# The load of the last two z1 tiles is queued on GpSimd behind the accumulating store of the fourth output tile

## The chip, the cores and the metric

The kernel runs on one NeuronCore of a Trainium2 chip, in one launch. The metric is the time of the program on the device in microseconds; of several runs the median is given. Five engines work side by side, each through its own instructions in order: TensorE (PE, matmuls and transposes, with its weight loads shown as PEld), VectorE (DVE), ScalarE (ACT), GpSimd (POOL) and SyncE (SP). SP only issues transfers here; ACT and POOL issue some as well. All transfers (DMAs) run on 16 DMA engines. What SP issues is on queue 1 of the profile, what POOL issues on queue 0.

## The reference

```python
def ref(x, wqkv, w_phi, wo, w_in, w_sp, b_sp, w_out):   # x: 1 x 2048 x 512, 32 heads of 16, FH = 688
    xn = layernorm(x)
    # A: linear attention with a learned feature map
    q, k, v = split_heads(xn @ wqkv)
    phi = lambda t: concat(softmax(t @ w_phi), softmax(-(t @ w_phi)))
    kv, z = phi(k).T @ v, sum(phi(k))
    a = (phi(q) @ kv) / (phi(q) @ z + 1e-6)
    # B: gated MLP that mixes over the sequence
    zz = gelu(xn @ w_in)
    z1, z2 = zz[..., :688], layernorm(zz[..., 688:])
    g = w_sp @ z2 + b_sp                                 # 2048 x 2048 times 2048 x 688
    b = (z1 * g) @ w_out
    return x + a @ wo + b
```

All is float32. The kernel splits each float32 operand of a matmul into a rounded part and a rest ("h" and "l") and does three matmuls (lines L57, L58, L59) for one.

## The kernel before

The sequence is cut into 16 tiles of 128 rows (NT = 16), taken in pairs for the mixing over the sequence (NP = 8 pairs).

The first part normalizes and transposes x, projects q, k, v and the first half of z (`z1_raw`), and puts the unfinished z1 (before its gelu) and the features of q to DRAM (`z1_d`, `e_d`). The second part makes z2. The third, up to about 486 us of the profile, multiplies `w_sp` with z2 pair by pair (tiles `g`); `drain` (L805 to L810) puts the sums together, and `gate` takes the gelu of the pair's z1 (L819), multiplies (L822), and returns a function `turn` that transposes the product in blocks (L831, L833) and stores it to DRAM as `u_d` and `ur_d` (L837, L839), from SP except for pair 6, where it is POOL. `load_z1` (L787) fetches a pair's z1: two transfers of 344 KB, issued on POOL. The last pair (7, tiles 14 and 15) is drained at the end of this part, but gated only in the middle of the next.

The last part, the loop over i = 0, 2, ..., 14 at the end of the function, makes the output tiles, two in a turn:

- `fetch_u` and `gated` bring u of a tile back (L855, L856) and split it on ACT and DVE (`uh`, `ul`); `project_u` multiplies it with `w_out` (tiles `wu`) into the PSUM tile `pout` (its last two matmuls are L1018).
- `load_q` brings the features of a q tile (`et`, L557); `features` ends them on DVE (`q_fin`, L564 to L571, with a last multiply L571); up to tile 7 the matrix engine transposes them (`ptq`, L989), from tile 8 on DVE does it in blocks and they go through DRAM (`q_d`, L580 and L582).
- `attend` multiplies with `kvT` (`po`, L1004) and splits the result (`oT`, first half on ACT, rest on DVE); `project_o` multiplies it with `wo` into the same `pout`, copies it to `xr` on ACT (L1040) and adds it to the output in DRAM with an accumulating store on POOL (L1041). x itself was put there earlier.
- before the loop, SP issues the loads of `kvT` (L972), of `wo` in 16 pieces of 64 KB (L850, tiles `wof`, rounded to `woh` and `wol`), and then `et` of tile 3, u of tiles 2 and 3, and `et` of tile 4.

After the turn i = 2 the z1 of the last pair is loaded, and after i = 6 (`GATE_LAST`) that pair is gated; its u is needed by the last turn.

The order of each engine's instructions is written by a scheduler that reckons with the times of instructions and transfers; the program text is only its input, so an instruction can come earlier than its place in the text. `with tc.issue_after(ins)` adds an edge: instructions of the block that are on the same engine as `ins` are put behind `ins` in that engine's order. It adds no wait on another engine. `lasts` is a list of remembered instructions for such edges; `lasts[6]` is read at one place only, the load of the last pair's z1.

Of the kernel before, what the change touches and what calls it, by code (L numbers as in the profile page):

```python
# [13 lines left out]
ALU = mybir.AluOpType  # L14
# [27 lines left out]
def mixer(ctx: ExitStack, tc: tile.TileContext, x, x_t, wv, wqkT, phi_bd, wo, w_in, wst, b_r, w_out, out):  # L42
    nc = tc.nc
    pe, act, dve, pool, sp = nc.tensor, nc.scalar, nc.vector, nc.gpsimd, nc.sync
# [10 lines left out]
    def mm3(dst, a, b, start, stop):  # L55
        (ah, al), (bh, bl) = a, b
        pe.matmul(dst, ah, bh, start=start, stop=False)  # L57
        pe.matmul(dst, ah, bl, start=False, stop=False)  # L58
        return pe.matmul(dst, al, bh, start=False, stop=stop).ins  # L59
# [500 lines left out]
    def q_fin(et, tmp, zb):  # L560

        e, r, t, w = et[:, :NF], *(et[:, NF + k * 2 * H:NF + (k + 1) * 2 * H] for k in range(3))
        den = et[:, NF + 6 * H:QW]
        dve.tensor_tensor(tmp, e, zb, op=ALU.mult)  # L564
        dve.tensor_reduce(t, heads(tmp), axis=AX.X, op=ALU.add)
        dve.tensor_tensor(t, t, r, op=ALU.mult)
        dve.scalar_tensor_tensor(den, pairs(t, 0), EPS_DEN, pairs(t, 1), op0=ALU.add, op1=ALU.add)
        dve.reciprocal(den, den)
        dve.tensor_tensor(w.rearrange("p (h a) -> p h a", a=2), r.rearrange("p (h a) -> p h a", a=2),
                          den.unsqueeze(2).to_broadcast([P, H, 2]), op=ALU.mult)  # L570
        return e, dve.tensor_tensor(heads(e), heads(e), bc(w, 2 * H), op=ALU.mult).ins  # L571
# [6 lines left out]
    def turn_q(s, dst, e, eng):  # L578

        dve.transpose(dst.rearrange("p (m c t) -> p m c t", c=NB, t=BL), e.rearrange("p (c m j) -> p m c j", c=NB, j=BL))  # L580
        for b in range(P // BL):
            eng.dma_start(q_d[s, :, b * QB:(b + 1) * QB].rearrange("(m j) w -> j m w", j=BL),  # L582
                          dst[b * BL:(b + 1) * BL].rearrange("p (m w) -> p m w", w=QB))
# [154 lines left out]
    for s in range(NT):  # L738
# [8 lines left out]
        for k, q in p:  # L747
            ins = act.activation(z[(slice(None), *k)], q, AF.Gelu_apprx_tanh, scale=r_x[:, s:s + 1]).ins
# [95 lines left out]
    def slot(name, dt=F32):  # L844
        return xz_tile(2 * FH, dt, name)
# [28 lines left out]
    lasts, wu = [None] * 9, []  # L874
# [67 lines left out]
    def er_pair(name):  # L942
        return cw.tile([P, 2, NF], F32, tag="er", bufs=3, name=name)

    def features(s):
        with tc.issue_after(fin[-1]):
            tmp = slot("qtmp")[:, :NF]
            es[s], ins = q_fin(ets.pop(s), tmp, zb)
        fin.append(ins)
        if s >= TQ:  # L950
            if s % 2 == 0:
                ft[s] = er_pair("f")
            turn_q(s, tmp, es.pop(s), pool)
            brought[s] = sp.dma_start(ft[s - s % 2][:, s % 2], q_d[s]).ins
            return
        lasts[6] = ins

    def gated(u):
        return split_u(*u, wk.tile([P, KF, P], F32R, tag="uh", name="uh"), wk.tile([P, KF, P], F32R, tag="ul", name="ul"))
# [61 lines left out]
    def project_o(i, oT, p):  # L1021
        ts = slice(i % 2 * P, (i % 2 + 1) * P)
        rows = slice(i * P, (i + 1) * P)
        xr = wk.tile([P, D], F32, tag="xr", bufs=3, name="xr")
        if i >= NT - 2:
            sp.dma_start(xr, x[rows, :])
        if i == NT - 1:
            dve.tensor_tensor(xr, p, xr, op=ALU.add)
            parts = [(slice(k * D // 2, (k + 1) * D // 2), pst.tile([P, D // 2], F32, tag="tr", name="pend")) for k in range(2)]
        else:  # L1030
            parts = [(slice(0, D), p)]
        for cs, q in parts:
            for c in range(ND):
                lasts[4] = mm3(q, (oT[0][:, c, ts], oT[1][:, c, ts]), (wo_h[:, c, cs], wo_l[:, c, cs]),
                               q is not p and c == 0, c == ND - 1)
            if i == NT - 2:
                dve.tensor_tensor(xr, p, xr, op=ALU.add)
                sp.dma_start(out[rows, :], xr)
            elif q is p:
                act.activation(xr, p, AF.Copy)  # L1040
                ins = pool.dma_start(out[rows, :], xr, accum_op=ALU.add).ins  # L1041
                tc.add_manual_dep(ins, seeds[i].name, mybir.DependencyInfo(
                    mybir.DependencyClass.Sync, mybir.DependencyReason.DATA), reason="out holds x")
            else:
                dve.tensor_tensor(xr[:, cs], q, xr[:, cs], op=ALU.add)
                sp.dma_start(out[rows, cs], xr[:, cs])
# [8 lines left out]
    with tc.issue_after(lasts[0]), tc.issue_after(lasts[1]), tc.issue_after(fin[-1]):  # L1055
        for c in range(ND):
            rows = [(m * QP, (m + 1) * QP) for m in range(c // 2 * 8 + c % 2, (c // 2 + 1) * 8, 2)]
# [7 lines left out]
    def ahead(i):  # L1065

        if i + 5 < NT:
            ets[i + 5] = load_q(i + 5, slot("et"))
        if i + 4 < NT:
            with tc.issue_after(brought[i + 2]) if i + 6 >= NT else ExitStack():  # L1070
                us[i + 4] = fetch_u(i + 4)
        if 3 < i + 3 < NT:
            features(i + 3)

    p, nxt = {}, dict(enumerate(uT))
    for i in range(0, NT, 2):
        p[i] = project_u(i, nxt.pop(i))
        if 0 < i < NT - 2:
            nxt[i + 2] = gated(us.pop(i + 2))
        with tc.issue_after(lasts[2]):  # L1080
            oT = attend(fT)
        with tc.issue_after(lasts[3]):
            p[i + 1] = project_u(i + 1, nxt.pop(i + 1))
        if not i:
            fin.append(lasts[7])
            features(3)
            with tc.issue_after(fin[-1]), tc.issue_after(lasts[8]):
                nxt[2] = gated(us.pop(2))
        if i < NT - 2:
            with tc.issue_after(fin[-1]) if not i else ExitStack():  # L1090
                nxt[i + 3] = gated(us.pop(i + 3))
        for k in range(2):
            project_o(i + k, oT, p.pop(i + k))
            ahead(i + k)
        if i == 2:
            with tc.issue_after(lasts[6]):
                z = load_z1(NP - 1)
        if i == GATE_LAST:
            with tc.issue_after(lasts[0]), tc.issue_after(lasts[1]):
                gate(NP - 1, cb, z, z, gt.tile([P, 2, FU], F32, tag="zt", name="zt"))()  # L1100
            p2.close()
        if i + 2 < NT:
            with tc.issue_after(lasts[4]):
                fT = attend_T(i + 2)
# [33 lines left out]
```

## Time and profile before

| | us |
|---|---|
| median of 3 runs | 617.96 |
| lowest and highest of them | 616.56, 618.06 |
| the profiled execution, its own time | 615.26 |
| its span, first to last instruction | 613.6 |
| z1 load of the last pair issued on POOL | 479.41 and next |
| last products of the third part end, first `pout` starts | 486.81 |
| accumulating store of tile 3 issued on POOL | 520.53 |
| gelu of the last pair on ACT | 546.53 |
| last `po` group on PE starts | 599.35 |

The granted TensorE clock was 1.000 of full speed over the whole span. Times in the profile are microseconds from the span's start. A row of the timeline gives start, length, engine, line, operation, the tile written and the tile read, the number of like instructions in a row, and in brackets how long the engine had been idle before it and what ended that. A row of the waits gives who waited for whom, the total, how often, and the longest. "POOL out" with L1041 is the accumulating store, "POOL z1t" with L787 the load in question.

### The profile page before, as it was taken

To read this page: it belongs to the slowest core of one execution; us is meant where nothing else is said; L and a number is where in the kernel's file an instruction comes from. 1 tells how busy PE (TensorE), PEld (TensorE's weight loads), DVE (VectorE), ACT (ScalarE), POOL (GpSimd) and SP (SyncE) were. 2 spreads that over 40 slices of the span, in tenths; PEclk is the share of its full clock that TensorE was granted. 3 is DMA by queue.
4 is the path that set the end of the run, shared out by engine and by line. 5 is a ranking of instruction groups with operands and counts; after the bars stand their busy time and mean duration, and the time that the engine had idled before them with its cause. 6 is when DMAs were issued, how large, how long until landed. Compare 5 with 4: busy or idle time off the path is not lost.

```text
span 613.6 us, 11385 instructions
## 1 busy us (share of the span) xinstructions
PE 606.3 (99%) x4286; PEld 551.5 (90%) x4286; DVE 519.9 (85%) x930; ACT 259.9 (42%) x414; POOL 132.4 (22%) x231
## 2 busy tenths in 40 slices
PE   8999999999999999999999999999999999999997
PEld 7888888888888999999999999999999978777776
DVE  5999999999988588999989897787779979999932
ACT  5653334423433547887434443332435243332220
POOL 4122232333111014542000002001100131053440
PEclk9999999999999999999999999999999999999999
DMA  8557776666547848001454746455566798599882
GB/s 309 196 135 170 224 174 183 153 161 171 134 120 206 275 155 308 2 1 35 150 135 133 193 100 182 132 158 145 162 179 215 239 312 253 150 293 278 222 221 67
DMA packets 57950, 107.85 MB, mean 176 GB/s; under 512 B 12392, under 2 KB 24552, under 8 KB 57672
## 3 DMA queue, kind: packets, MB, share of 16 engines
q1 hardware_dynamic: 43656, 65.22, 34.5%
q0 software_dynamic: 11936, 36.28, 24.0%
q10 hardware_dynamic: 2304, 5.64, 2.4%
q8 instruction: 33, 0.54, 0.4%
q14 instruction: 21, 0.17, 0.1%
HBM read 66.85 MB, written 35.54 MB: 167 GB/s over the span
## 4 chain that ended last, share of the span: by engine, by line
PE 83%; DVE 6%; DMA 6%; issue 2%; SPq 1%; ACT 1%; POOL 0%; ACTq 0%; DVEq 0%; POOLq 0%
PE g L57 8%; PE g L58 8%; PE g L59 8%; PE proj L58 7%; PE proj L57 7%; PE proj L59 7%; PE zps L58 6%; PE zps L59 6%; PE zps L57 6%; PE pout L57 5%; PE pout L59 5%; PE pout L58 5%; DVE A L53 2%; DMA wf<-in_wst 1%; PE po L1004 1%
## 5 line engine op out<-in xcount | busy, mean ns | idle before, releaser
L57 PE MATMUL g<-B,A 128*128 128x344 f32 x448 | 142.5, 319 | 0.3 <-DVE c L810 0.3
L58 PE MATMUL g<-B,A 128*128 128x344 f32 x448 | 142.4, 319 | 0.0
L59 PE MATMUL g<-B,A 128*128 128x344 f32 x448 | 138.9, 318 | 0.0
L57 PEld LDWEIGHTS g<-B,A 128*128 128x128 f32 x448 | 84.0, 188 | 0.9 <-DVE c L810 0.6
L58 PEld LDWEIGHTS g<-B,A 128*128 128x128 f32 x448 | 84.0, 188 | 0.0
L59 PEld LDWEIGHTS g<-B,A 128*128 128x128 f32 x448 | 83.6, 188 | 0.0
L49 ACT ACTIVATE A<-S 128x512 fp32r<-128x512 f32 x64 | 39.4, 628 | 70.7 <-DVE S L622 52.3
L57 PE MATMUL proj<-wqk_h,xT 128*128 128x512 f32 x128 | 50.1, 391 | 0.0
L59 PE MATMUL proj<-wqk_h,xT 128*128 128x512 f32 x128 | 49.8, 389 | 0.0
L58 PE MATMUL proj<-wqk_l,xT 128*128 128x512 f32 x128 | 49.8, 389 | 0.0
L125 ACT ACTIVATE e<-e,r_x 128x1024 f32<-128x1024 f32 x26 | 29.8, 1149 | 42.3 <-DVE e L124 41.3
L53 DVE TENSOR_TENSOR A<-S,A 128x512 fp32r<-128x512 f32 x64 | 43.0, 684 | 3.0 <-ACT A L49 2.8
L49 ACT ACTIVATE A<-wf 128x512 fp32r<-128x512 f32 (+1 forms) x64 | 32.8, 515 | 28.1 <-DMA wf<-in_wst 15.8
L57 PE MATMUL zps<-w1h,xT 128*128 128x344 f32 (+2 forms) x128 | 40.8, 320 | 0.0
L59 PE MATMUL zps<-w1h,xT 128*128 128x344 f32 (+2 forms) x128 | 40.7, 318 | 0.0
L58 PE MATMUL zps<-w1l,xT 128*128 128x344 f32 (+2 forms) x128 | 40.7, 318 | 0.0
L57 PE MATMUL zps<-w2h,xT 128*128 128x344 f32 (+2 forms) x128 | 40.7, 318 | 0.0
L58 PE MATMUL zps<-w2l,xT 128*128 128x344 f32 (+2 forms) x128 | 40.6, 317 | 0.0
L59 PE MATMUL zps<-w2h,xT 128*128 128x344 f32 (+2 forms) x128 | 40.3, 317 | 0.0
L53 DVE TENSOR_TENSOR A<-wf,A 128x512 fp32r<-128x512 f32 (+1 forms) x64 | 35.1, 550 | 4.1 <-ACT A L49 4.0
L787 POOL DMA_DIRECT2D z1t<-z_d x16 | 8.7, 550 | 132.5 <-DMA wf<-in_wst 98.1
L128 DVE TENSOR_REDUCE sm<-e 128x64 f32<-128x1024 f32 x26 | 31.1, 1199 | 2.5 <-ACT e L125 2.5
(219 smaller groups left out, 1434.4 us busy)
## 6 DMA issues: line engine op xcount, KB each, us to landing
wf<-in_wst SPq DMA_DIRECT2D x64, 256.0 KB, 3.4
e_d<-e POOLq DMA_DIRECT2D x16, 544.0 KB, 5.0
et<-e_d SPq DMA_DIRECT2D x16, 544.0 KB, 7.6
z_d<-z1f ACTq DMA_DIRECT2D x16, 344.0 KB, 3.1
z1t<-z_d POOLq DMA_DIRECT2D x16, 344.0 KB, 4.6
zacc<-e POOLq DMA_DIRECT2D x10, 512.0 KB, 4.8
u<-u_d SPq DMA_DIRECT2D x15, 320.0 KB, 5.8
xt<-in_x SPq DMA_DIRECT2D x16, 256.0 KB, 4.4
```

The source lines that it names most:

```text
L49: return act.activation(h, src, AF.Copy).ins
L53: return (eng or dve).tensor_tensor(l, src, h.bitcast(F32), op=ALU.subtract).ins
L57: pe.matmul(dst, ah, bh, start=start, stop=False)
L58: pe.matmul(dst, ah, bl, start=False, stop=False)
L59: return pe.matmul(dst, al, bh, start=False, stop=stop).ins
L125: softmax_pair.last = less, act.activation(e, e, AF.Exp, scale=scale).ins
L128: dve.tensor_reduce(sm, heads(e), axis=AX.X, op=ALU.add)
L787: pool.dma_start(t[:, k, :FH], z1_d[2 * i + k])
L1004: lasts[3] = pe.matmul(po[r][c * QP:(c + 1) * QP, k], kvT[rows, m // 2, cols], fs[m // 4][rows, m // 2 % 2], start=True, stop=True).ins
```

## The change

The remembered instruction `lasts[6]` is no longer the last one of `features` (a multiply on DVE) for the q tiles below 8, but the accumulating store of `project_o` (on POOL). At the place where it is read, after the turn i = 2, the latest such store is that of output tile 3, the fourth. The two transfers of the z1 load are thereby queued on POOL behind that store. Nothing else differs.

```diff
     def features(s):
         with tc.issue_after(fin[-1]):
             tmp = slot("qtmp")[:, :NF]
             es[s], ins = q_fin(ets.pop(s), tmp, zb)
         fin.append(ins)
         if s >= TQ:
             ...
             return
-        lasts[6] = ins

     def project_o(i, oT, p):
             ...
             elif q is p:
                 act.activation(xr, p, AF.Copy)
-                ins = pool.dma_start(out[rows, :], xr, accum_op=ALU.add).ins
+                lasts[6] = ins = pool.dma_start(out[rows, :], xr, accum_op=ALU.add).ins
                 tc.add_manual_dep(ins, seeds[i].name, ...)

         # the place where it is read, unchanged
         if i == 2:
             with tc.issue_after(lasts[6]):
                 z = load_z1(NP - 1)
```

## Prediction

> **What bounds the kernel now.** I read the page's busy shares first, then the list of waits of the matrix engine, then the chain of work that ended last over the stretch where it leaves the matrix engine, then the queues of GpSimd and SyncE in that stretch.
>
> ```profile
> PE 606.3 (99%) x4286; PEld 551.5 (90%) x4286; DVE 519.9 (85%) x930; ACT 259.9 (42%) x414; POOL 132.4 (22%) x231
> PE ptq L989 <- DVE et L571: 1.0, 1, 1.0
> PE pout L57 <- ACT oT L49: 0.2, 1, 0.2
> PE pout L57 <- DVE c L810: 0.2, 1, 0.2
> ```
>
> The first row is of the page: matmul is busy 606.3 of 613.6 us. The other three are all the waits of the matrix engine (total, times, longest) between 475 us and the end. The changed transfer can act only there, so everything that can be won in the tail is 1.0 + 0.2 + 0.2 = 1.4 us, unless an order of instructions changes. The chain of work that ended last (start, length, what) goes through the longest of the three:
>
> ```profile
> 479.66 0.42 SPq L856
> ...
> 480.17 6.96 DMA kvT<-kvT_d
> ...
> 491.71 0.43 SPq L850
> ...
> 492.24 6.33 DMA et<-e_d
> ...
> 498.58 1.24 DVE qtmp L564
> ...
> 502.24 1.24 DVE et L571
> ...
> 503.52 1.53 PE ptq L989 x12
> ```
>
> Read backwards: the transposes `ptq` of query tiles 2 and 3 wait for `features(3)` (lines L564 to L571 on VectorE), that for the load `et` of tile 3, that for its turn on SyncE's queue behind the last pieces of `wo` (L850), and those for the landing of `kvT`, which took 6.96 us for 256 KB. So a slow stretch of the transfers between 480 and 487 us is passed on to the matrix engine at 503.5. Here is what was under way:
>
> ```profile
> 479.41 1.07 POOL L787 DMA_DIRECT2D z1t<-z_d  x2 [23.89 <-DVE ul_rt L53]
> 490.01 2.35 POOL L837 DMA_DIRECT2D u_d<-z1t  x4 [9.53 <-DVE z1t L833]
> SPq L850 <- DMA u<-u_d: 2.4, 1, 2.4
> SPq L850 <- DMA kvT<-kvT_d: 0.4, 1, 0.4
> SPq L850 <- DMA u<-ur_d: 0.3, 1, 0.3
> z1t<-z_d POOLq DMA_DIRECT2D x2, 344.0 KB, 5.9
> q0 software_dynamic: 160, 0.70, 24.6%
> ```
>
> The first two rows are of GpSimd in order of time, the next three the waits of SyncE's queue between 479 and 488 us, the last two the transfers of the same 9 us (issues with their median us to landing; then a queue's packets, MB and share of the 16 engines). Queue 0 is GpSimd's: its 160 packets are the two z1 loads, 0.70 MB. SyncE stood 2.4 + 0.3 + 0.4 = 3.1 us before its L850 loads, waiting for three earlier loads to land. Within 482 to 485 us alone:
>
> ```profile
> q0 software_dynamic: 141, 0.63, 60.6%
> q1 hardware_dynamic: 266, 0.35, 33.2%
> ```
>
> The z1 loads had 60.6% of the engines' time while SyncE's loads (queue 1) had 33.2%.
>
> **The change part by part.**
>
> The edge that is removed. It tied the z1 load to the last multiply of `features(6)`, an instruction of VectorE; the load is issued on GpSimd.
>
> ```profile
> 520.17 1.22 DVE L571 TENSOR_TENSOR et<-et 128x1024 f32<-128x1024 f32 x1
> ```
>
> That multiply (the fifth in order from tile 2's) starts at 520.17, 41 us after the load was issued at 479.41: the old edge holds nothing back. Removing it costs and brings 0.
>
> The edge that is added. Now the accumulating store of output tile 3 is the instruction remembered, and it is on GpSimd, as the load is.
>
> ```profile
> 520.53 0.86 POOL L1041 DMA_DIRECT2D out<-xr  x1 [0.78 <-ACT xr L1040]
> 535.84 0.60 POOL L582 DMA_DIRECT2D q_d<-qtmp  x1 [14.45 <-DVE qtmp L580]
> 546.53 1.34 ACT L819 ACTIVATE z1t<-z1t 128x1376 f32<-128x1376 f32 x1
> ```
>
> So both issues move from 479.41 to 520.53 + 0.86 = 521.4, past eight stores of `u_d`/`ur_d` (from 490.01; they wait for VectorE's transposes, not for the load) and four output stores. The two issues cost GpSimd 1.07 us there, inside 14.45 us in which it idles: 0. What is queued behind is the `q_d` store at 535.84, 13 us after them. With the 5.9 us to landing seen above, z1 is there at about 528.4; its only reader in wait is the gelu at 546.53, 18 us later: 0. Without that cover ScalarE would stop at the gelu, and behind it `xr` of tiles 6 and 7, `uh` and `oT`, which feed the matrix engine.
>
> What leaves 479 to 486 us. 24.6% of 9 us is 2.2 us of all 16 engines. From below: 0, if SyncE's loads landed no sooner without it. From above: the whole 2.2 us (SyncE's 3.1 us of waits leave room). I take the part that lies in 482 to 485, just ahead of the landings that SyncE waited for: 60.6% of 3 us = 1.8 us. Then the last L850 and `et` of tile 3 are issued 1.8 us earlier, at 490.4.
>
> What that is worth. These rows decide:
>
> ```profile
> 495.09 0.63 ACT L49 ACTIVATE woh<-wof 128x512 fp32r<-128x512 f32 x1 [2.63 <-DMA wof<-in_wo]
> 496.36 1.28 DVE L53 TENSOR_TENSOR oT<-po,oT 128x512 fp32r<-128x512 f32 x2
> 498.58 1.23 DVE L564 TENSOR_TENSOR qtmp<-et,zb 128x1024 f32<-128x1024 f32 x1 [0.94 <-DMA et<-e_d]
> 501.89 0.60 PE L989 MATMUL ptq<-ident,et 128*128 128x128 f32 x4
> 503.52 1.53 PE L989 MATMUL ptq<-ident,et 128*128 128x128 f32 x12 [1.04 <-DVE et L571]
> ```
>
> With its 6.33 us to landing unchanged, `et` is there at 490.4 + 6.3 = 496.7. VectorE is then free at 497.64 (496.36 + 1.28) less what the last `woh` gains; that rounding waited 2.63 us for a `wo` piece, of the same queue, so it moves by the same 1.8 us and VectorE is free at 495.8. `features(3)` starts at 496.7 in place of 498.58, ends at 501.7 in place of 503.48, and the matrix engine, which reaches the second group of transposes at 501.89 + 0.60 = 502.5, no longer waits: 1.04 us. The same earlier `woh` lets `oT` be rounded earlier, which ends the 0.18 us in which `pout` waited for it (the second wait of the list). If only `et` came sooner and `oT` not, the gain would be VectorE's 0.94 us; if nothing came sooner, 0. The third wait, 0.2 us for L810, is a drain of the matrix engine's own products and stays.
>
> What is late next. After 503.5 VectorE has no pause until 586, so it could be the next to hold the matrix engine up:
>
> ```profile
> 510.00:586.00 76.00, 76.00 (x483) 59.92 (x484) 74.45 (x112) 24.00 (x40) 25.10 (x39) 1.00 0.84 237
> 513.99 0.63 DVE L53 TENSOR_TENSOR oT<-po,oT 128x512 fp32r<-128x512 f32 x1
> 514.83 0.39 PE L59 MATMUL pout<-woh,oT 128*128 128x512 f32 x1
> ```
>
> The first row is a stretch of 76 us with the busy times of PE, PEld, DVE, ACT, POOL: VectorE 74.45. The other two show the low part of `oT` ready at 514.62 and first used at 514.83, a margin of 0.2 us. VectorE's run of work starts with `features(3)`, so it moves forward by 1.8 us while the matrix engine moves by 1.2: the margin holds. It would be lost, and the gain cut to what VectorE gained plus 0.2, if `features(3)` moved by less than 1.0.
>
> What arrives at 521 to 528 us. The 2.2 us of transfers now compete with `et` loads of tiles 10 and 11 and the stores of output tiles 2 and 3:
>
> ```profile
> 530.00:535.00 5.00, 5.00 (x24) 4.09 (x23) 4.90 (x8) 0.98 (x2) 0.00 (x0) 1.00 0.11 39
> 519.03 2.62 SPq L557 DMA_DIRECT2D et<-e_d  x2
> 538.96 1.22 DVE L564 TENSOR_TENSOR qtmp<-et,zb 128x1024 f32<-128x1024 f32 x1
> ```
>
> The transfer engines are 0.11 busy between 530 and 535, so the queue is empty again soon after, and `et` of tile 10, issued at 519.03, is first read at 538.96. A delay of 2.2 us is hidden: 0. That cover is 20 us less a landing of some 7.
>
> [...] GpSimd's issue moves into the stretch where VectorE is 74.45 of 76 us busy. The stores issued there between 495 and 530 us, by this row of L1041, landed after:
>
> ```profile
> DMA to landing us min/median/max: 6.5/7.4/9.3
> ```
>
> By the longest, z1 lands at 521.9 + 9.3 = 531.2, still 15 us ahead of the gelu, and the sum stays. [...]
>
> **The sum.** 1.04 + 0.18 = 1.22 us off the profiled execution's own 615.26 (span 613.6), so 614.04, or 0.20%. The median of the runs shown is 617.96, 2.7 us above the profiled execution; 0.2% off it is 616.75, forecast as 616.8.
>
> **The rivals.**
>
> First, nothing is won: the loads on SyncE's queue land as before, because they are bound by something else than the z1 packets, or `et` issued at 490.4 now shares the engines with the `u_d` stores from 490.01 and lands at 498.5 again; or the scheduler leaves the load where it is. For it: those stores are in flight there. Against it: 60.6% in 482 to 485, and only 1 us of the 1.8 is needed. Time 617.96.
>
> Second, slower, by one mechanism: the gate of the last z1 pair on VectorE is put at another place. The order of instructions comes from a scheduler that reckons with times, and z1 now becomes ready 42 us later.
>
> ```profile
> 550.67 1.58 DVE L822 TENSOR_TENSOR z1t<-z1t,c 128x1376 f32<-128x1376 f32 x1
> 554.41 0.32 DVE L833 STREAM_TRANSPOSE zt<-z1t 128x192 f32<-128x192 f32 x1
> 560.14 1.28 DVE L53 TENSOR_TENSOR oT<-po,oT 128x512 fp32r<-128x512 f32 x2
> ```
>
> The block from 550.67 to 554.73, 4.1 us with what lies between, is now early in its iteration. Put just ahead of the next `oT` (560.14), it delays the matrix engine by up to 4.1 less a margin like the 0.2 above, 3.9; with the 1.2 won, +2.7: 620.7. It decides from 1.2 us of delay on. Against it: the gelu is queued behind `uh` of tile 9 in both kernels, and z1 is there before that in both.
>
> [...]
>
> **How the numbers follow.** Forecast 0.65, nothing won 0.22, the gate moved 0.10, GpSimd held up 0.03. The forecast's own range is 0.9 to 1.4 us, 616.5 to 617.1, and the runs before scatter from 616.56 to 618.06, so a median may lie 1.3 us lower: 615.2. Upwards the range takes in nothing won (617.96) and the third rival: 618.6. Outside it is the second, 0.10, and some scatter. About 0.3% (1.85 us) is what a measurement of this kernel can tell from no change: faster means under 616.1, which the forecast reaches with scatter in about 3 of 10 cases, 0.2; slower is the second rival, 0.1; the rest, 0.7.
>
> **What would show it.** Right: the z1 load at about 521 us, behind the output store of tile 3; SyncE's wait at L850 for `u` well under 2.4 us; `kvT` landed in about 5 us in place of 6.96; `et` of tile 3 issued near 490.4; no wait of `ptq` for L571; the gelu without a wait for z1. Wrong: the load still near 479; the 1.04 us still there, or a new wait of `pout` for `oT` of about the same size; the gate's multiply at another place among VectorE's instructions.

## The result and the profile after

| | before | after |
|---|---|---|
| median, 6 runs each side by side | 616.35 | 613.06 |
| lowest and highest | 615.79, 618.06 | 612.58, 614.60 |
| the profiled execution, its own time | 615.26 | 613.14 |
| its span | 613.6 | 611.4 |

The ratio is 0.9946, with a 95% interval of 0.9927 to 0.9965: 3.3 us less, where 1.2 were forecast. 613.06 lies below the forecast's range (615.2 to 618.6). Of the 3.7 us between the forecast of 616.8 and 613.06, 2.1 are the size of the gain and 1.6 the start: three of the six runs of before are those of the section "Time and profile before", with a median of 617.96, and over all six it is 616.35. The two profiled executions differ by 2.1 us only.

The order of instructions is the same on TensorE, VectorE, ScalarE and SyncE; on GpSimd only the two z1 loads have moved, behind the eight stores of u and four output stores. Line numbers after L956 are one less in the kernel after (L1041 is L1040 there, L989 is L988, L1004 is L1003).

The page of after, its busy shares and the split of the chain that ended last:

```profile
span 611.4 us, 11387 instructions
PE 605.8 (99%) x4286; PEld 551.9 (90%) x4286; DVE 519.9 (85%) x930; ACT 259.7 (42%) x414; POOL 132.4 (22%) x231
PE 96%; DVE 1%; DMA 1%; issue 0%; POOL 0%; ACT 0%; POOLq 0%
```

and that last row on the page of before:

```profile
PE 83%; DVE 6%; DMA 6%; issue 2%; SPq 1%; ACT 1%; POOL 0%; ACTq 0%; DVEq 0%; POOLq 0%
```

The busy time of TensorE has hardly moved (605.8 against 606.3 us). What has changed is the chain: the detour through SyncE's queue, the landing of `et` and VectorE is gone, and 96% of the span is now matmul behind matmul.

The place of the change, in after: GpSimd's timeline with the z1 landings, SyncE's timeline with its waits between 479 and 488 us that concern the loads, and the one queue that moved anything between 482 and 485 us.

```profile
518.44 0.86 POOL L1040 DMA_DIRECT2D out<-xr  x1 [0.78 <-ACT xr L1039]
518.99 1.45 POOL L787 DMA_DIRECT2D z1t<-z_d  x2
DMA to landing us min/median/max: 8.0/8.2/8.3
480.28 8.01 SPq L850 DMA_DIRECT2D wof<-in_wo  x16
488.38 1.66 SPq L557 DMA_DIRECT2D et<-e_d  x1
SPq L850 <- DMA kvT<-kvT_d: 0.8, 1, 0.8
q1 hardware_dynamic: 418, 0.60, 62.4%
```

In those 3 us SyncE's queue moved 0.60 MB in place of 0.35, and queue 0 nothing. The 16 pieces of `wo` are issued within 8.01 us; in before that row reads

```profile
480.60 11.54 SPq L850 DMA_DIRECT2D wof<-in_wo  x16
```

so `et` of tile 3 is issued at 488.38 in place of 492.24, 3.9 us sooner (0.3 of it because SyncE comes to `kvT` at 479.85 in place of 480.17).

What that does to the engines, in after (timelines of ScalarE, VectorE and TensorE):

```profile
491.70 1.09 ACT L49 ACTIVATE oT<-po 128x512 fp32r<-128x512 f32 x2
497.47 1.22 DVE L571 TENSOR_TENSOR et<-et 128x1024 f32<-128x1024 f32 x1
486.44 0.47 PE L57 MATMUL pout<-wu,u_uh 128*128 128x512 f32 x1
495.55 0.39 PE L57 MATMUL pout<-woh,oT 128*128 128x512 f32 x1
501.04 1.91 PE L988 MATMUL ptq<-ident,et 128*128 128x128 f32 x16
506.79 1.09 PE L1003 MATMUL po<-f,kvT 64*32 64x256 f32 x32
```

`oT` is rounded by 492.79, 2.8 us ahead of the matmul that needs it (495.55), and `features(3)` is done at 498.69, 2.3 us ahead of the transposes (501.04). Both waits are gone. The list of TensorE's waits from 475 us to the end has no row in after.

From the first `pout` matmul to the second group of `po` TensorE needs 506.79 - 486.44 = 20.35 us. In before the same two stand at

```profile
486.81 0.47 PE L57 MATMUL pout<-wu,u_uh 128*128 128x512 f32 x1 [0.16 <-DVE c L810]
508.87 1.09 PE L1004 MATMUL po<-f,kvT 64*32 64x256 f32 x32
```

22.06 us apart. These 1.7 us of the 2.1 between the two profiles come from the stretch that the change touches. Most of the rest, 0.37, was there when the stretch began; 0.27 of it dates from a wait at 463 us, ahead of where the change can act. Below, "the stretch" is always this distance.

### The profile page after: what moved, and what is told of

Its sections match the earlier page's. It is cut to its first block, busy times and chain, and to the rows that moved or that the text cites. A ratio compares the mean times of both kernels' runs of the same rounds, so it can differ in the third digit from the quotient of the medians.

```text
span 611.4 us, 11387 instructions
## 1 busy us (share of the span) xinstructions
PE 605.8 (99%) x4286; PEld 551.9 (90%) x4286; DVE 519.9 (85%) x930; ACT 259.7 (42%) x414; POOL 132.4 (22%) x231
## 4 chain that ended last, share of the span: by engine, by line
PE 96%; DVE 1%; DMA 1%; issue 0%; POOL 0%; ACT 0%; POOLq 0%
PE g L57 12%; PE g L58 11%; PE g L59 11%; PE proj L57 7%; PE proj L58 7%; PE proj L59 7%; PE zps L57 6%; PE zps L59 6%; PE zps L58 6%; PE pout L57 6%; PE pout L59 5%; PE pout L58 5%; PE po L1003 1%; PE pout L1017 1%; DMA zacc<-e 1%; PE kvps L373 1%
```

## The experiments

The theory: the two z1 transfers at 479 us take the 16 DMA engines from SyncE's loads, SyncE's queue stands, and `oT` and `et` of tile 3 are late for TensorE. The rivals: it is the new place of the load, and not its absence from 479 us, that helps; or the profile's 1.7 us are all that the stretch gives, and the rest of 3.3 us comes from elsewhere.

**The dose.** Both kernels again, and two between and beyond them, on one chip. Half of the load moved:

```diff
 # after, at the load of the last pair's z1
-    z = load_z1(NP - 1)
+    z = gt.tile([P, 2, FH + REM], F32, tag="z1", name="z1t")
+    pool.dma_start(z[:, 0, :FH], z1_d[2 * (NP - 1)])           # stays at 479 us
     with tc.issue_after(lasts[6]):
+        pool.dma_start(z[:, 1, :FH], z1_d[2 * (NP - 1) + 1])   # behind tile 3's store
```

Twice the load at 479 us (the second pair lands in a tile that is overwritten later, so it is pure traffic):

```diff
 # before, right behind the z1 load
+    zt = gt.tile([P, 2, FU], F32, tag="zt", name="zt")
+    for k in range(2):
+        pool.dma_start(zt[:, k, :FH], z1_d[2 * NP - 4 + k])
...
```

> The changed kernel again, beside the others of this call. Theory A: 0.993 to 0.997 of before, no wait of ptq or of pout for oT between 495 and 504 us. Rival B: nearer to 1.000 than 0.997, with the difference from before scattered over the whole span.

> The kernel before, unchanged, for a second profile and for how far two sets of runs of one program differ. Theory A (the z1 load of 0.70 MB at 479 us delays SyncE's loads of u, kvT and wo, and through them the load of et 3 and the transposes ptq): the profile shows again waits of the matrix engine for L571 (ptq) and for oT between 495 and 504 us, and the ratio is 1.000 within 0.002. Rival B (the gain lies elsewhere, in waits before 479 us that differ from one execution to the next): the wait at 463.85 for L810 or others before 479 differ by as much as what the change gained, and the ptq wait may be missing.

> One of the two z1 transfers (344 KB) stays at 479 us, the other is queued behind the accumulating store of tile 3. Theory A: about half of the delay is left: SyncE waits some 1.5 us at the wo loads in place of 3.1, the ptq wait is between 0 and 0.5 us, and the time is 0.994 to 0.998 of before (nearer to after, since the first microsecond of delay is hidden). Rival B: no relation to the amount; 1.000.

> The kernel before, with a second pair of transfers of the same size behind the z1 load at 479 us (z1 of tiles 12 and 13, into the tile that the gate later overwrites). Theory A: another 2.2 us of all transfer engines lies ahead of kvT and wo, so et 3 is issued 1.5 to 2.2 us later than before, the ptq wait grows from 1.0 to about 3 us, and the time is 1.002 to 1.005 of before. Rival B: 1.000.

| z1 bytes at 479 us | median us | ratio to before (616.51) | 95% | stretch in the profile, us |
|---|---|---|---|---|
| 0 (after again) | 614.03 | 0.9959 | 0.9938 to 0.9980 | 20.30 |
| 344 KB (half) | 615.61 | 0.9977 | 0.9961 to 0.9993 | 22.09 |
| 688 KB (before again) | 617.64 | 1.0010 | 0.9992 to 1.0029 | 23.59 |
| 1376 KB (double) | 618.62 | 1.0018 | 1.0002 to 1.0034 | 26.35 |

The medians rise with the bytes at each step, and the stretch with them. The intervals of half and double lie clear of before on either side (double's only just); those of double and before again overlap. One profile of each could not carry this order alone: half's stretch of 22.09 us is no shorter than the 22.06 of before's first profile. And of the 2.8 us from before again to double, 2.7 have no wait in them (from the first product with `oT` to the transposes 8.31 us against 5.61); the clock was halved there, as the last section shows. From the end of the stretch to the end of the kernel all four take the same, 104.7 to 105.1 us.

The ratio of half came as expected, but not the way to it: SyncE stood 3.0 us at the `wo` loads, where 1.5 were expected, and the wait of `ptq` was 0.9 us and not 0.5 at the most. In double it was the wait for `oT` that was long, and not the one of `ptq`.

TensorE's waits within the stretch, of half, of before again and of double:

```profile
PE ptq L988 <- DVE et L571: 0.9, 1, 0.9
PE pout L57 <- ACT oT L49: 0.4, 1, 0.4
```

```profile
PE pout L57 <- ACT oT L49: 2.9, 1, 2.9
```

```profile
PE pout L57 <- ACT oT L49: 3.2, 1, 3.2
```

The second fence is the surprise: it is the kernel before, unchanged, and the wait that was 0.18 us in the profile that the prediction was made from is 2.9 us here, while the one at `ptq` is absent. ScalarE and TensorE in that execution:

```profile
497.29 0.63 ACT L49 ACTIVATE woh<-wof 128x512 fp32r<-128x512 f32 x1 [2.82 <-DMA wof<-in_wo]
497.82 1.07 ACT L49 ACTIVATE oT<-po 128x512 fp32r<-128x512 f32 x2
498.46 0.50 PE L57 MATMUL pout<-woh,oT 128*128 128x512 f32 x1 [2.85 <-ACT oT L49]
```

The last rounding of `woh` waited 2.82 us for its piece of `wo` and started at 497.29, where it started at 495.09 in the first profile; `oT` is queued behind it on ScalarE, and TensorE stood until then.

**Is the place behind tile 3 special?** The edge of after read one turn earlier (behind tile 1's store) or one later (behind tile 5's):

```diff
 # after, in the loop over i, where lasts[6] is read
-        if i == 2:
+        if i == 0:        # behind_tile1;  i == 4: behind_tile5
```

> The changed kernel, with the z1 load queued behind the accumulating store of output tile 1 in place of tile 3, so at about 502 us, where the transfer engines are fully busy (a share of 1.05 in before). Theory A (only the stretch from 479 to 495 us counts; any later place is hidden): 0.993 to 0.997 of before, as the changed kernel within 0.001. Rival D (it is the gap in the transfers behind tile 3's store that makes the place good): slower than the changed kernel by 0.002 or more, with new waits of VectorE or the matrix engine between 502 and 512 us.

> The changed kernel, with the z1 load queued behind the accumulating store of output tile 5, so at about 536 us; it should land 4 to 6 us ahead of the gelu at 544. (On SyncE the eight stores of the last pair's u stand in a slightly other order.) Theory A: 0.993 to 0.997 of before, as the changed kernel within 0.001. Rival D: other than the changed kernel by 0.002 or more.

Behind tile 1: 614.13, ratio 0.9936 (0.9911 to 0.9961), stretch 20.31 us, no wait in it: after within the intervals. So between these two places nothing depends on the place, only on the load being away from 479 us. Behind tile 5: 615.93, ratio 0.9966 (0.9942 to 0.9991), against the expectation. Six of its twelve executions took 613.58 to 614.77 us, as after does, and six 617.10 to 618.43; the profile is of one of the latter. Its stretch is as short, 20.32 us, but two new waits stand later, in ScalarE's and TensorE's timelines. The z1 load and its landing, the landing of the `q_d` stores of tile 9 behind it, the load of these features (`f`) on SyncE, and the two waits:

```profile
537.26 1.64 POOL L787 DMA_DIRECT2D z1t<-z_d  x2
DMA to landing us min/median/max: 10.6/10.9/11.2
539.06 2.21 POOL L582 DMA_DIRECT2D q_d<-qtmp  x4 [0.16 <-issue]
DMA to landing us min/median/max: 10.3/11.0/11.7
552.52 0.32 SPq L954 DMA_DIRECT2D f<-q_d  x1
549.05 1.35 ACT L819 ACTIVATE z1t<-z1t 128x1376 f32<-128x1376 f32 x1 [3.51 <-DMA z1t<-z_d]
550.31 1.32 ACT L1039 ACTIVATE xr<-pout 128x512 f32<-128x512 f32 x2
557.23 1.11 PE L1003 MATMUL po<-f,kvT 64*32 64x256 f32 x16 [2.12 <-issue]
```

and of after, the same stores' landing and the same load of `f`:

```profile
DMA to landing us min/median/max: 7.0/7.2/7.4
547.10 0.32 SPq L954 DMA_DIRECT2D f<-q_d  x1
```

z1 lands by 549, and the gelu waits 3.51 us for it: that is the cover that the prediction named, used up. But TensorE's 2.12 us, for which the profile names no cause, do not come from the `xr` copies behind the gelu: those had ended at 551.63, and TensorE worked on until 555.1. They come by GpSimd's queue. The `q_d` stores of tile 9 stand right behind the z1 load and take some 4 us longer to land than in after; SyncE waits for them, so it issues the load of `f` at 552.52 in place of 547.10. By the trace's record of landings `f` was there at 557.14, just ahead of the product at 557.23; in after it was there at 551.45, 2.3 us ahead of that product. (A few of SyncE's u stores stand in another order in this kernel.)

**Each of the two waits by itself.** First, in before, the rounding of `oT` ahead of the last quarter of `wo` on ScalarE and VectorE, so that `oT` no longer waits for `wo`; second, in before, the load of `et` of tile 3 ahead of `kvT` and `wo` on SyncE:

```diff
 # before; oT_first: the last of the wo tiles is only loaded in its loop (wo_t), and rounded behind oT
...
+        if not i:
+            with tc.issue_after(lasts[8]), tc.issue_after(lasts[7]):
+                round_h(act, wo_h[:, ND - 1], wo_t)
+                wo_rest = rest_l(wo_l[:, ND - 1], wo_t, wo_h[:, ND - 1])
...
 # before; et_first: ahead of the loads of kvT and wo
+    et3 = slot("et")
+    et3_in = sp.dma_start(et3[:, :NF + 2 * H], e_d[3]).ins
...
 # the loads of wo are put behind et3_in; the old load of et of tile 3 is gone
```

> The kernel before, with z1 still loaded at 479 us; on ScalarE and VectorE the first oT is split ahead of the last quarter of wo (woh, wol) in place of behind it; the transfers are the same. Theory A1: the wait of the matrix engine for oT at 496 us (0.2 us in one profile of before, 2.9 us in the other) is oT standing in ScalarE's queue behind the last woh, which stands for a wo piece that came late. Then pout starts on wo at 496.1 without that wait and meets a shorter one, under 1 us, at the last quarter; the ptq wait for L571 of 1 to 1.5 us stays, since et 3 is as late as before; executions with a mean clock of 0.997 or less, 19 of 47 before, become rare; ratio 0.996 to 0.999. Rival B1: the matrix engine needs the late wo data itself at that point, so the order on ScalarE changes nothing: same wait, same share of executions with a lowered clock, 1.000.

> The kernel before, with z1 still loaded at 479 us; on SyncE's queue the load of et 3 (544 KB) stands ahead of kvT and the 16 pieces of wo in place of behind them. Theory A2 (what counts is the sum of transfers that lie ahead of each reader): et 3 has landed by 489 us and the ptq wait is gone, but kvT and wo come about 1.7 us later, so the wait for oT grows by 1 to 1.7 us and the clock is lowered in more executions than before; ratio 0.999 to 1.005. Rival B2 (the place of et 3 in SyncE's queue is the cause, as my prediction had it, and the rest is hidden): the ptq wait goes and no other grows, 0.997.

`oT_first`: 617.54 against 617.62, ratio 0.9994 (0.9972 to 1.0016). `et_first`: 618.72, ratio 1.0018 (1.0001 to 1.0036). TensorE's waits in the stretch, of the one and of the other:

```profile
PE ptq L989 <- DVE et L571: 2.7, 1, 2.7
```

```profile
PE pout L57 <- ACT oT L49: 3.3, 1, 3.3
```

The wait that the edit aims at is gone in each, and the other one has grown to take its place. For `et_first` that is what was expected (A2, 0.999 to 1.005). For `oT_first` a part of the gain was expected (0.996 to 0.999) and a `ptq` wait that stays at 1 to 1.5 us; the gain did not show, and the wait was 2.7. `oT` and `et` are two outlets of one delay: SyncE's pieces of `wo` and `et` of tile 3 are in the same queue, behind the same slow stretch. The longer TensorE stands at the first (`oT`), the later it reaches the second, and the less it stands there (in the table below 2.1 to 2.9 us at `oT` with none at `ptq`, 0.2 or 0.3 with 1.0 to 1.4); in one profile (before_e) it stands long at both (1.8 and 1.1 us).

**How much differs between executions of before.** The unchanged kernel five times more, one profile each:

> The kernel before, unchanged, one more profile. Theory A3: the waits for oT and ptq between 495 and 504 us add up to 1.2 to 3.5 us, and where one of them is 3 us or more the granted clock is 0.5 in the slices behind it. Rival B3: a lowered clock at another place, or without such a wait.

> The kernel before, unchanged, one more profile. Theory A3: as for the other: waits for oT and ptq of 1.2 to 3.5 us together, and a clock of 0.5 only behind a wait of about 3 us. Rival B3: a lowered clock at another place, or without such a wait.

> The kernel before, unchanged. 52 of its 93 timed executions had a mean clock of 0.997 or less, but none of its four profiles. Theory A4: where the mean is 0.997, the half clock stands in one stretch of about 3.4 us right behind a wait for oT or ptq between 496 and 506 us, as in the profiles of the kernels double_early, et_first and oT_first, and the matrix engine loses some 1.7 us there. Rival B4: the half clock of before stands elsewhere (at the start, in the w_sp part, at the end), and has nothing to do with the z1 load.

> The kernel before, unchanged, one more profile. Theory A4: a half clock, where there is one, stands behind a wait for oT or ptq between 496 and 506 us. Rival B4: it stands elsewhere.

> The kernel before, unchanged, one more profile. Theory A4: a half clock, where there is one, stands behind a wait for oT or ptq between 496 and 506 us. Rival B4: it stands elsewhere.

| execution | first `pout` | second `po` group | stretch | waits in it | its time |
|---|---|---|---|---|---|
| before (the prediction's) | 486.81 | 508.87 | 22.06 | `oT` 0.2, `ptq` 1.0 | 615.26 |
| before again | 486.45 | 510.04 | 23.59 | `oT` 2.9 | 616.85 |
| before_b | 488.86 | 511.43 | 22.57 | `oT` 0.3, `ptq` 1.4 | 617.86 |
| before_c | 488.99 | 511.18 | 22.19 | `oT` 0.3, `ptq` 1.1 | 617.64 |
| before_d | 486.12 | 508.94 | 22.82 | `oT` 2.1 | 615.43 |
| before_e | 485.93 | 509.70 | 23.77 | `oT` 1.8, `ptq` 1.1 | 616.50 |
| before_f | 488.46 | 512.99 | 24.53 | `oT` 2.3 | 619.36 |
| after, after again, behind tile 1 | 486.44, 488.05, 487.89 | 506.79, 508.35, 508.20 | 20.35, 20.30, 20.31 | none | 613.14, 614.72, 614.55 |

The stretch is 20.3 us in each execution without the load, and 22.06 to 24.53 with it, 23.08 in the mean of the seven: 2.8 us more. The two timed comparisons of after gave 3.3 and 2.5 us, behind tile 1 gave 3.5. The prediction's profile was the one of seven that lost least in the stretch. The first column scatters as well, from 485.9 to 489.0, in both kernels: that comes from waits ahead of 479 us and is no part of the change. The half clock stood where A4 put it, behind the wait of before_f; but that wait was 2.3 us, and A3 had it only behind some 3 us.

**A shorter wait, by other work.** Eight useless matmuls in before between the second product with `w_out` and the first with `wo`, so that TensorE would stand for a shorter time and its clock would stay up:

```diff
 # before, in the first turn, ahead of the products with wo
+            t = pst.tile([P, 2, 2, P], F32, tag="tr", name="fill").rearrange("p a k b -> p (a k b)")
+            for k in range(8):
+                with tc.issue_after(lasts[2]):
+                    lasts[2] = pe.matmul(t, wu[0][0][:, :P], wu[0][0], start=True, stop=True, skip_group_check=True).ins
...
 # the first product with wo is put behind the last of them
```

> The kernel before, with z1 still loaded at 479 us, and eight matmuls of 128x512 without use (a product of two pieces of wu into a free PSUM tile, some 1.9 us) between the second u product and the first product with wo, where the matrix engine waits for oT. (In the turns after that, VectorE, SyncE and GpSimd have some instructions in another order.) Theory A3: before loses its time at two places, the waits for oT and for ptq, which come from the same late transfers and stand in for one another, and on top of it the granted clock falls to half for some 3 to 6 us when the matrix engine has stood still for about 3 us. The fill shortens the pause without delaying what follows by much, since ptq has to wait for et 3 anyway: executions with a mean clock of 0.997 or less, 40 of 76 of before, become rare, and the time is 0.997 to 1.000 of before. Rival B3: the lowered clock of some executions has nothing to do with the pause: as many as before, and the time 1.000 to 1.003.

619.44, ratio 1.0032 (1.0011 to 1.0053), against the expectation. It can't be read as meant: the scheduler changed the order of VectorE, SyncE and GpSimd in later turns, and TensorE has a wait of 1.8 us there that before hasn't. Whether the filling by itself would have paid stays open. The clock did as expected: its mean was at or under 0.997 in 2 of 12 timed executions, and in 12 of 17 of before beside it.

## Why the prediction was wrong in size and right in its mechanism

**Right.** The place (the load came at 518.99, behind tile 3's store, 2.4 us before the predicted 521.4, mostly because all before it had moved up). The contention (SyncE no longer waits for u in after's profile, and for 0.5 to 1.1 us in the three other profiles without the load, against 2.4; `kvT` landed 4.4 us after its issue in place of 6.96). The path from SyncE's queue to `oT`, `et`, `features(3)` and the two waits. VectorE's margin: TensorE has no new wait after 503 us, and the low part of `oT`, 0.2 us ahead of its use in before, is 1.9 us ahead in after (ready at 510.82, used at 512.74). The third wait of the list, for L810, was said to stay; it is absent from after and from the six other profiles of before, and there in `half_early` (0.2) and behind tile 5 (0.4), so it comes and goes without the change. The cover of the moved load: it landed in 8.2 us in place of the 5.9 taken, and ScalarE's row

```profile
544.44 1.34 ACT L819 ACTIVATE z1t<-z1t 128x1376 f32<-128x1376 f32 x1
```

has no idle time for it, 17 us after the landing. 8.2 us lies in the 6.5 to 9.3 of the stores that the prediction went by; the slowest z1 load, behind tile 5, took 11.2.

**The rivals.** "Nothing is won" fell with the ratio and the dose. "The gate moved on VectorE" fell with VectorE's order, which is the same. "GpSimd held up", the third, fell with the landing just named: the upper end of the range, 618.6, rests on a z1 load that a busy VectorE holds back past the gelu, and no run shows that; with VectorE busy for 9.69 us of the 10 from 518 on, z1 landed in 8.2 us in after.

**Wrong: "everything that can be won in the tail is 1.0 + 0.2 + 0.2 = 1.4 us", and with it the sum of 1.04 + 0.18.** Both terms were the waits of one execution, and the stretch in which they lie lost 1.7 us there, the least of seven; the mean is 2.8 us. The terms were mis-sized in three ways.

- The wait for `oT`, 0.18 us in the sum, was 0.2 to 2.9 us in the seven profiles. It depends on when the last piece of `wo` lands against when TensorE arrives, and a landing among 0.70 MB of other traffic was not the same twice (the last rounding of `woh` behind it started at 495.09 and at 497.29). This is the largest part: with the one for `ptq`, 0 to 1.44 us, the listed waits of the stretch are 2.1 us in the mean of the seven, against 1.22.
- A wait as listed is shorter than the delay it makes, because the idle time is counted from the modelled end of the matmul before, and without a wait the next starts ahead of that end (in after, the first product with `oT` starts 0.16 us ahead of it); also, the matmul behind a wait takes longer (0.50 us in place of 0.39 there). Between the two profiles the starts of the same matmuls move apart by 0.45 us at the wait of 0.18, and by 1.24 at the one of 1.04: 1.7 us in place of 1.22.
- A long wait is followed by a lowered clock in some executions (next section but one): 1.7 us in one of the seven, so some 0.25 in the mean.

The profile could have warned: it took 615.26, 2.7 us less than the median of 617.96 in the table that the prediction started from. The prediction took 0.2% off the median as if the 2.7 us were spread over everything; about 1 us of them was in just the stretch that the change empties (23.08 - 22.06).

**Mis-sized without harm:** the shift of `et` of tile 3, 1.8 us taken with 2.2 as the most, was 3.9. The 16 pieces of `wo` were issued in 3.5 us less; SyncE stood 0.8 us before them for an earlier landing in place of 3.1. That standing time was the better bound than the share of the engines.

Left open: the waits ahead of 479 us, which make the start of the stretch scatter by 3 us.

## What to carry to other kernels

The wait for a transfer that competed with another was a draw from a spread here (0.2 to 2.9 us for `oT` in seven executions); before such a length is put into a sum, look at how far the profiled execution stands from the median of the runs, and take the profile's waits as a lower bound where it is among the fastest (1.22 us listed, against 2.1 in the mean of seven). Move a bulk load that is not urgent out of a stretch in which a queue of urgent ones is being filled: its place afterwards did not matter until it came so late that its reader waited for it (3.51 us, behind tile 5), and that stores queued right behind it, soon needed by TensorE, landed late too (11.0 us in place of 7.2). And where two engines waited for loads of one queue, curing one wait showed the other (2.7 us in `oT_first`, 3.3 in `et_first`); cure the queue.

## What the hardware showed besides

TensorE's granted clock fell to half after some of these waits. The windows of before_f (length, then busy us and instructions of PE, PEld, DVE, ACT and POOL, the granted clock, the DMA share, GB/s), and TensorE's first product with `oT` there:

```profile
500.02 0.50 PE L57 MATMUL pout<-woh,oT 128*128 128x512 f32 x1 [2.30 <-ACT oT L49]
498.00:500.00 2.00, 0.00 (x0) 0.00 (x0) 0.49 (x1) 1.15 (x3) 0.00 (x0) 1.00 0.96 322
500.00:502.00 2.00, 1.98 (x6) 1.59 (x7) 2.00 (x4) 0.75 (x2) 0.00 (x0) 0.73 1.04 375
502.00:504.00 2.00, 2.00 (x6) 1.59 (x5) 1.93 (x3) 1.18 (x2) 0.00 (x0) 0.50 1.04 376
504.00:506.00 2.00, 2.00 (x9) 1.60 (x9) 1.86 (x5) 0.16 (x1) 0.00 (x0) 0.92 1.06 282
```

and one window of before again, whose wait was longer (2.9 us):

```profile
502.00:504.00 2.00, 2.00 (x10) 1.64 (x9) 1.83 (x6) 0.60 (x1) 0.42 (x1) 1.00 1.16 321
```

Busy is 2.00 us of 2.00 in both, but 6 matmuls fit in place of 10: only the column of the clock tells. The price in before_f: it is 2.02 us behind after at the first `pout` (488.46 to 486.44), 4.47 at the first product with `oT` (500.02 to 495.55), and 6.20 at the second `po` group (512.99 to 506.79). The last 1.7 us have no wait in them.

The half clock lasted 3.41 us, or twice that in the profile of the double load. It came behind waits of 2.1 (behind tile 5), 2.3 (before_f), 2.7 (`oT_first`), 3.2 and 3.3 us (double, `et_first`), and not behind 2.1 in before_d or 2.9 in before again, so the length of the wait alone doesn't decide it.

The place of the wait in the traces separates the two groups. In each profile that has a half clock, the times between two changes of the granted clock are whole multiples of 3.413 us (in before_f 494.933, 3.413 and 112.640: 145, 1 and 33 of them; the one time at full clock that the traces of before's first profile and of after list, 607.572 and 604.159, is 178 and 177 of them). So in these profiles the clock changed only at the borders of a grid, wherever the waits lay. Cut along that grid into cells of 3.41 us, each fall to half followed a cell in which TensorE stood for 1.95 us or more: 1.95 behind tile 5, 2.15 in double, 2.30 in before_f, 2.72 in `oT_first`, 3.28 in `et_first`. Cells with 1.81 us (before again) or 1.76 (`filled`) were followed by none. Two cells of before_f, and two of before again, across whose border the wait of 2.9 us lay:

```profile
497.51:500.93 3.42, 1.12 (x5) 0.75 (x5) 1.42 (x3) 1.61 (x3) 0.00 (x0) 1.00 0.99 338
500.93:504.34 3.41, 3.41 (x10) 2.67 (x9) 3.27 (x6) 1.47 (x2) 0.00 (x0) 0.50 1.03 368
494.00:497.41 3.41, 1.60 (x8) 0.97 (x6) 0.69 (x1) 0.59 (x2) 0.00 (x0) 1.00 0.88 235
497.41:500.83 3.42, 2.37 (x10) 1.98 (x11) 2.88 (x4) 2.23 (x4) 0.00 (x0) 1.00 1.02 347
```

That is read from sixteen profiles; no kernel was made to test it. Waits alike in length could thus end differently: the 2.3 us of before_f lay in one cell, and the 2.9 us of before again in two, with 1.81 us in the first. Where between 1.81 and 1.95 us of standing the limit lies, if it is one, was not tried.

Mean clocks at or under 0.997 were had by 52 of 93 timed executions of before and by 1 of 18 of after. The gain does not rest on this: among the executions with a mean clock above 0.997 alone, the medians of the set in the dose table were 616.25 (before) and 613.52 (after), still 2.7 us apart.
